# Batch 1 of a fused cross-attention and Fourier-mixing kernel: its second set of scores is turned from the first, and its steps are put in another order

## The chip, the cores and the metric

The kernel runs on one core of a Trainium2 chip. The time is device microseconds of one launch, the median of ten runs: 299.51 us, from 299.33 to 301.87. The core has five engines that each work through a list of instructions in order: TensorE (PE in the profile, its weight loads PEld), VectorE (DVE), ScalarE (ACT), GpSimd (POOL) and SyncE (SP), which here only issues DMAs. Engines wait for each other by semaphores, so an instruction that waits holds up everything behind it on its own engine.

## The reference, cut to what matters

For each of 8 batches, 8 heads of 512 rows `x` and 32 rows `state` attend to each other. The 544 result rows of 512 columns go through a two-dimensional Fourier transform, of which the real part is kept, then a normalisation and a two-layer network.

```
scores  = scale * x @ state.T        ; a  = softmax(scores)  ; xread = a  @ state    # 512 rows
scores2 = scale * state @ x.T        ; a2 = softmax(scores2) ; sread = a2 @ x        # 32 rows
X   = concat(xread, sread)           # per head; heads side by side give (8, 544, 512)
u   = X + real(fft(fft(X, axis=1), axis=2))
un  = (u - mean(u)) / sqrt(var(u) + 1e-6)
out = u + relu(un @ w_ch1) @ w_ch2   # w_ch1 512 x 2048, w_ch2 2048 x 512
```

`scores2` is the transpose of `scores`, so one exponential serves both softmaxes if it is turned.

## The kernel before, in words

Every engine's order is written out by hand; nothing is rescheduled. The kernel handles a batch in three stages, and interleaves the stages of neighbouring batches so that PE has always something to do.

**Attention** (`attend(b)`; batch 0 has its own `open_batch`). `turn_state` and `turn_x` (for batch 1 together `turn_all`, with three copies `copies1` out of PSUM) make `sT` and `xT`, the transposes of state and x. Batches from 2 on get them by DMA transposes on SP's queue (L377, L388). `scores(i)` (L432, PSUM tile `esp`) makes rows of x by columns of state and their exponential `E` on ACT (L437). The turned form `ET` is needed for `xread`. Batches from 2 on get it by `turn_scores(g)`: `E` times an identity or a mirrored identity (L444, tile `eTp`), copied by ACT with a row sum as a by-product (`sums`, L445). Batch 1 computes its scores a second time the other way round in `scores_t(g)` (L421) and takes a second exponential (L423). Then come the reads, a list called `r1` for batch 1 and `R` for batch 2. `r1[0]` and `R[0]` are `read_low` (L457 into `xrp`, a GpSimd copy `XT` at L514); index 2 and, for batch 1, 3 or 5 are the forward reads `xfp`; `sread_heads` (batch 1, L493) or `sread_by_head` (later, L477) is the state's read `srp`; `state_rows` (batch 1, L508) gathers the heads into rows; the last entry is the other mirrored read followed by the folds on DVE (L529 to L549), which make the input `XQ` of the transform. `sread_heads` takes the state's softmax sums from eight matmuls with one column each (L497).

**Transform** (`transform(b)`, list `T` for batch 2). `over_s` (L788, tile `gp`) is the transform along rows, `over_d` (L684 and L685, tile `yp`) along columns; `add`, `centre` and `turn_u` add x, subtract the mean and turn the result into `unT`, the input of the network. Batches 0 and 1 turn on PE (L856), later ones by DMA (L852).

**Network**. `layer1` is `L` for batch 0 (16 quarter steps of 16 small matmuls, L941) and `L1` for batch 1 (16 steps of 4 matmuls, L931). `layer2` gives `M` (16 steps of 4 matmuls, L996, 4 steps for each of 4 row tiles). Every fourth step of `layer2` ends with a store: DVE makes `ot` (L963), SP writes it. What is left of `M` at batch 1, `M[7]` to `M[15]`, is called `M1[0]` to `M1[8]`.

PSUM has three buffers for `esp`, `eTp`, `tp`, `gp`, `yp` and `srp` together (pool psQ), three for the network's `ph` and `po` (psF) and one pair for the reads (psX). A tile that takes a buffer waits until the one before it has been read.

One chain of orders and waits outside PE matters here. GpSimd clears and fills the state blocks of batch 2 once its DMA has landed (L168), makes the matrix `mirror` (L100, L101), issues the first half of w2 (L325, `second_weights(0, 2)`), copies and folds the low rows of batch 1 (L514 to L526), issues the second half of w2, and later casts x of batch 2 (L1123). The last four columns of that cast come only after w2's last part has landed (the read of w2 at L1181 serves for that wait). SP's DMA transposes of x of batch 2 (L388) wait for that cast, the loads of x of batch 3 stand behind these on SP's queue (L145), and GpSimd's cast of batch 3 (L148) waits for the loads. Behind that cast on GpSimd stands the copy `XT` of batch 2 (L514), and DVE may not overwrite the low rows (L484) before it is done.

Of the kernel before, what the change touches and what calls it, by code (L numbers as in the profile page):

```python
# [15 lines left out]
AF = mybir.ActivationFunctionType  # L16
# [14 lines left out]
def kernel(  # L31
# [8 lines left out]
    nc = tc.nc  # L40
    B, H, S, D = x.shape
# [316 lines left out]
    turned = {}  # L358

    def attend(b):  # L360
# [52 lines left out]
        copies = []  # L413


        def scores_t(g):
            p = qt("eTp")
            for cols, rows in ((slice(0, 128), slice(0, 128)), (slice(128, 256), slice(255, 127, -1)),
                               (slice(256, 416), slice(256, 416)), (slice(416, 512), slice(511, 415, -1))):
                for hp in range(2):  # L420
                    nc.tensor.matmul(p[:, cols], lhsT=sT[:, 2 * g + hp, :], rhs=xT[:, 2 * g + hp, rows],  # L421
                                     start=(hp == 0), stop=(hp == 1))
            nc.scalar.activation(ET[:, g, :], p, AF.Exp, scale=scale)  # L423


        def scores(i):
            p = qt("esp")
            for si in (2 * i, 2 * i + 1):
                for pr in range(4):
                    hp = pr % 2  # L430
                    o = (si % 2) * 256 + pr * 64
                    nc.tensor.matmul(  # L432
                        p[:, o:o + 64].rearrange("p (h j) -> p h j", j=Ns),
                        lhsT=xT[:, pr, si * 128:(si + 1) * 128],
                        rhs=sT[:, pr, 64 * hp:64 * hp + 64].rearrange("p (h j) -> p h j", j=Ns)[:, :, ::-1 if b < 2 else 1],
                        start=True, stop=True)
            nc.scalar.activation(E[:, 2 * i:2 * i + 2].rearrange("p a b c -> p (a b c)"), p, AF.Exp, scale=scale)  # L437

# [48 lines left out]
        def sread_heads():  # L487
            p = qt("srp")
            for g in range(2):
                for si in range(4):  # L490
                    for hh in range(4):
                        c0 = 1 + 256 * g + 64 * hh
                        nc.tensor.matmul(p[32 * hh:32 * hh + 32, 64 * g:64 * g + 64], lhsT=E[:, si, g, 32 * hh:32 * hh + 32],  # L493
                                         rhs=xin[:, si, c0:c0 + 64], start=(si == 0), stop=(si == 3))
            for g in range(2):
                for si in range(4):
                    nc.tensor.matmul(p[:, 128 + g:129 + g], lhsT=E[:, si, g, :], rhs=xin[:, si, 0:1], start=(si == 0), stop=(si == 3))  # L497
            rcs = wk.tile([128, 2], F32, name="rcs", tag="rcs")
            nc.vector.reciprocal(rcs, p[:, 128:130])
            nc.vector.tensor_tensor(XQ[:, 0:2 * D].rearrange("p (g d) -> p g d", g=2),  # L500
                                    in0=p[:, 0:128].rearrange("p (g d) -> p g d", g=2),
                                    in1=rcs.unsqueeze(2).to_broadcast([128, 2, D]), op=ALU.mult)

        def state_rows():
            p = qt("hdp")
            pv = p[0:32, :].rearrange("p (h g d) -> p h g d", h=4, g=2)
            for hh in range(4):
                nc.tensor.matmul(pv[:, hh], lhsT=ident[:, 32 * hh:32 * hh + 32], rhs=XQ[:, 0:2 * D].rearrange("p (g d) -> p g d", g=2),  # L508
                                 start=True, stop=True)
            nc.scalar.copy(XR[0:32, 0, 512:0:-1].rearrange("p (g h d) -> p h g d", g=2, d=D), pv)  # L510

# [44 lines left out]
        if b < 2:  # L556
            first = [turn_state, lambda: turn_x(0), lambda: turn_x(1)]
            if b == 1:
                first = [turn_all] + [lambda i=i: copies[i]() for i in range(3)]
            first += [lambda: scores_t(0), lambda: scores_t(1),  # L560
                     lambda: scores(0), lambda: scores(1)]
        else:
            first = [lambda: scores(0), lambda: scores(1), lambda: turn_scores(1), lambda: turn_scores(0)]
            if b >= x_by_dma:
                turned[b] = lambda: (b > 2 and turn_state(), turn_x(0), turn_x(1))
                turned[b, 0] = turn_state
            else:
                first = [turn_state, lambda: turn_x(0), lambda: turn_x(1)] + first
# [562 lines left out]
    keep_low()  # L1131
    clears(1)
    clear_state(2, 3)
    state_blocks(2, 3, nc.gpsimd.tensor_copy)
    make_mirror()
    clear_state(3, 4)
    nc.gpsimd.tensor_tensor(gate, xs_of[0][:, 0:4], w1[:, :, 3 * 512], op=ALU.add)
    second_weights(0, 2)
# [2 lines left out]
    turned[2, 0]()  # L1141
    load_state(3, 4, s_dram)
    turn_u(0, 1)
    add_sums(0, 0)
    centre_sums(0, 0)
    copies1[0]()
    copies1[1]()
    warm(4)
    L[0]()
    s1[0]()  # L1150
    copies1[2]()
    L[1]()
    turn_u(0, 0)
    s1[1]()
    add_sums(1, 1)
    centre_sums(1, 1)
    add_sums(1, 0)
    L[2]()
    s1[2]()
    r1[0]()  # L1160
    r1[1]()
    r1[2]()
    nc.gpsimd.tensor_copy(gate, xs_of[2].rearrange("p (i c) -> p i c", i=4)[:, :, 0])
    second_weights(2, 4)
    clear_state(4, B)
    L[3]()
    s1[3]()
    r1[3]()
    centre_sums(1, 0)
    L[4]()  # L1170
    r1[4]()
    r1[5]()
    turn_u(1, 1)
    L[5]()
    r1[6]()
    r1[7]()
    nc.gpsimd.tensor_copy(gate, XQs[1].rearrange("p (g j c) -> p g j c", g=2, j=4)[:, 1, 3, 0:4])
# [5 lines left out]
    turned[2]()  # L1183
    load_x(3)
    turn_in_dram(4, B)
    L[6]()
    L[7]()
    turn_u(1, 0, nc.scalar.copy)
    spread(0, 1)
    state_ones(2, B)  # L1190
    L[8]()
    L[9]()
    L[10]()
    L[11]()
    over_s1(0)
    over_s1(1)
    L[12]()
    over_s1(2)
    over_s1(3)
    keep_middle()  # L1200
    L[13]()
    over_d1(0)
    add1(0, 1)
    L[14]()
    centre1(0, 1)
    over_d1(1)
    add1(0, 0)
    L[15]()
    centre1(0, 0)
    add1(1, 1)  # L1210
    M[0]()
    turn_u1(0, 1, nc.scalar.copy)
    M[4]()
    centre1(1, 1)
    add1(1, 0)
    M[1]()
    turn_u1(0, 0, nc.scalar.copy)
    centre1(1, 0)
    M[5]()
    M[2]()  # L1220
    turn_u1(1, 1)
    M[6]()
    turn_u1(1, 0)
    spread(0, 0)
    done()
    for root in first_roots[0:1] + first_roots[5:6]:
        root()
    M[3]()
    done1()
    l2, scores_first = M, scores_next  # L1230
    for b in range(1, B + 1):
        reads_next = reads_after
        l2, l2_now = (layer2(b), [l2[7]] + l2[8:]) if b == 1 else (layer2(b) if b < B else [], l2)
        early, until, start = {2: (7, 0.25, 0.22), 3: (3, 0.13, 0.1)}.get(b, (0, 0, 0.08))
        l2_now = l2_now + (layer2(("L", b // 4)) if b in (3, 7) else [])
        streams = [(l2_now[:early], 0, until), (l2_now[early:], until + 0.02 if early else 0, 1)]
        if b == 1:
            M1, L1, R, T, s2 = l2_now, layer1(1), reads_next, transform(2), scores_first
            scores_next, reads_after = attend(3)
            s3 = scores_next  # L1240
            def spreads():
                spread(1, 1)
                spread(1, 0)
                for root in first_roots[6:8] + first_roots[1:5]:
                    root()

            for step in (M1[0], spreads, L1[0], M1[1], s2[0], s2[1], M1[2], L1[1], s2[2], s2[3], lambda: cast_x(3), turned[3], M1[3], L1[2],
                         lambda: load_state(4, B, s_dram), lambda: load_x(4), R[0], L1[3], R[1], R[2], L1[4], R[3], L1[5], R[4],
                         L1[6], R[6], L1[7], M1[4], R[7], L1[8], M1[5], M1[6], R[8], L1[9], L1[10], T[0], T[1], L1[11], T[2], T[3],
                         L1[12], T[4], L1[13], M1[7], T[5], s3[0], L1[14], T[6], s3[1], L1[15], T[7], T[8], s3[2], s3[3], T[9], T[10],  # L1250
                         T[11], M1[8], lambda: state_blocks(4, B, nc.gpsimd.tensor_copy)):
                step()
            continue
        if b < B:
            streams.append((layer1(b), start, 1))
        if b + 1 < B:
            reads, mix = {2: ((0.1, 0.45), (0.57, 0.88)), 3: ((0.03, 0.4), (0.5, 0.86))}.get(b, ((0, 0.375), (0.47, 0.85)))
            streams.append((reads_next, *reads))
            streams.append((transform(b + 1), *mix))
        if b + 2 < B:  # L1260
            scores_next, reads_after = attend(b + 2)
            streams.append(([lambda: (cast_x(b + 2), turned[b + 2]())], 0.2, 0.2))
            streams.append((scores_next, 0.5, 1))
        if b + 3 < B:
            streams.append(([lambda: load_x(b + 3)], 0.35, 0.35))
        if b in (3, 7):
            streams.append((low_rows(b // 4), 0.02, 0.2))
            streams.append((layer1(("L", b // 4)), 0.36, 0.8))
        weave(*streams)
# [30 lines left out]
```

## Time and profile before

| | |
|---|---|
| median of 10 runs | 299.51 us |
| the profiled execution, whole | 301.87 us |
| its span, first to last instruction | 300.1 us |
| PE busy | 286.7 us, 96% |
| DVE / ACT / POOL busy | 59% / 46% / 31% |
| granted TensorE clock | 1.000 |
| instructions | 6032 |

The profiled execution is the slowest of the ten runs; 1.77 us of it lie outside the span. Times in the profile count from the start of the span. An engine's row gives start and duration, and in brackets the idle time before it with the instruction or DMA that ended the wait. PE's matmuls overlap, so that a row's duration is longer than the distance to the next row; that distance is what a step costs.

### The profile page before, as it was taken

How to read it: one execution, taken by the hardware profiler on the slowest of the kernel's cores; microseconds unless marked ns; L12 is line 12 of the kernel's file. 1: busy time of each engine (PE TensorE's matmuls, PEld its weight loads, DVE VectorE, ACT ScalarE, POOL GpSimd, SP SyncE). 2: the span in 40 equal slices, each digit the busy share in tenths (PEclk: the TensorE clock that was granted, in tenths of full speed). 3: DMA queues.
4: the chain of work that ended last, by engine and by line, in shares of the span. 5: the costliest groups of instructions: out<-in, count | busy, mean ns of one | idle time of the engine just before them, and what ended most of it. 6: DMA issues, size and time to landing. Idle time of an engine off the chain costs nothing.

```text
span 300.1 us, 6032 instructions
## 1 busy us (share of the span) xinstructions
PE 286.7 (96%) x2302; PEld 164.7 (55%) x2333; DVE 178.1 (59%) x441; ACT 139.2 (46%) x258; POOL 91.8 (31%) x227
## 2 busy tenths in 40 slices
PE   5999999979899999999999999999999999999995
PEld 5789974435444655466544554455444544555443
DVE  8868987376768487645648394757568474011122
ACT  6888674635824662255423543354524443334200
POOL 6764943560580045301343033502240121000000
PEclk9999999999999999999999999999999999999999
DMA  9999993956954944574543865253332133500354
GB/s 157 191 203 189 143 168 64 181 141 142 171 119 94 207 107 72 124 171 110 91 100 72 179 123 125 52 119 75 89 88 55 37 87 90 122 14 21 98 128 126
DMA packets 110824, 34.86 MB, mean 116 GB/s; under 512 B 101980, under 2 KB 106332, under 8 KB 110796
## 3 DMA queue, kind: packets, MB, share of 16 engines
q1 hardware_dynamic: 100076, 28.72, 45.5%
q0 software_dynamic: 4224, 4.19, 9.5%
q10 hardware_dynamic: 6496, 1.57, 2.5%
q8 instruction: 18, 0.29, 0.5%
q14 instruction: 10, 0.08, 0.1%
HBM read 22.41 MB, written 14.02 MB: 121 GB/s over the span
## 4 chain that ended last, share of the span: by engine, by line
PE 75%; DMA 12%; POOL 4%; DVE 3%; SPq 2%; issue 2%; ACT 1%; ACTq 0%; POOLq 0%; DVEq 0%
PE po L996 33%; PE ph L931 32%; DMA w<-in_moe_w_ch_dram 4%; DMA s_dram<-in_state_dram 3%; PE gp L788 2%; DMA xs<-in_x_dram 2%; DMA gen<-s_dram 2%; SPq L145 2%; PE po L988 1%; PE eTp L444 1%; PE yp L685 1%; PE yp L684 1%; SPq L388 1%; DMA xT<-xin 1%; PE xrp L457 1%
## 5 line engine op out<-in xcount | busy, mean ns | idle before, releaser
L996 PE MATMUL po<-w,hT 128*128 128x512 bf16 x482 | 121.0, 379 | 1.2 <-issue 0.5
L933 ACT ACTIVATE hT<-ph 128x512 bf16<-128x512 f32 x112 | 66.9, 597 | 117.6 <-PE ph L931 113.5
L931 PE MATMUL ph<-unT,w 128*128 128x512 bf16 x431 | 112.0, 379 | 1.1 <-DVE ot L963 0.3
L931 PEld LDWEIGHTS <-w 128*128 128x128 bf16 x576 | 50.3, 98 | 46.8 <-issue 0.9
L996 PEld LDWEIGHTS <-hT 128*128 128x128 bf16 x496 | 46.7, 98 | 47.4
L963 DVE SCALAR_TENSOR_TENSOR ot<-po,rstd,U 128x512 f32<-128x512 f32 (+2 forms) x33 | 24.2, 733 | 50.4 <-PE po L996 47.9
L792 POOL COPY GL<-G 128x128 bf16<-128x128 bf16 x7 | 2.0, 289 | 73.4 <-ACT G L789 73.4
L337 DVE BATCH_NORM_STATS2 st<-U 128x6 f32<-128x512 f32 x32 | 21.8, 681 | 0.1
L689 DVE TENSOR_TENSOR U<-yp,XR 128x512 f32<-128x512 f32 x14 | 9.6, 683 | 19.9 <-PE yp L685 19.9
L344 POOL TENSOR_TENSOR rstd<-rstd,mhalf 128x1 f32<-128x1 f32 x34 | 20.0, 589 | 2.7
L343 POOL TENSOR_TENSOR rstd<-mv,epst 128x1 f32<-128x1 f32 x34 | 6.4, 189 | 44.7 <-DVE mv L339 44.7
L941 PE MATMUL ph<-unT,w 128*128 128x128 bf16 x256 | 16.2, 219 | 0.3 <-DVE unT L857 0.3
L941 PEld LDWEIGHTS <-w 128*128 128x128 bf16 x256 | 15.0, 98 | 0.5 <-issue 0.4
L789 ACT CAST G<-gp 128x288 bf16<-128x288 f32 x28 | 12.9, 482 | 5.1 <-PE gp L788 5.1
L148 POOL CAST xin<-xs 128x2048 bf16<-128x2048 f32 (+1 forms) x9 | 11.7, 1317 | 1.4 <-DMA xs<-in_x_dram 1.4
L943 ACT ACTIVATE hT<-ph 128x512 bf16<-128x512 f32 x16 | 9.5, 593 | 4.9 <-PE ph L941 4.8
L847 DVE TENSOR_SCALAR ub<-U,mv 128x512 bf16<-128x512 f32 x20 | 10.2, 511 | 0.9 <-DVE mv L339 0.3
L514 POOL COPY XT<-XR 32x514 bf16<-32x514 bf16 x7 | 4.3, 607 | 20.3 <-DVE XR L466 20.3
L466 DVE TENSOR_TENSOR XR<-xrp,rs 128x512 bf16<-128x512 f32 x14 | 9.7, 695 | 0.5
L466 DVE TENSOR_TENSOR XF<-xfp,rs 128x512 bf16<-128x512 f32 x14 | 9.7, 692 | 0.5
L465 DVE RECIPROCAL rs<-xrp 128x8 f32<-128x8 f32 x14 | 2.9, 206 | 11.2 <-PE xrp L457 11.2
L689 DVE TENSOR_TENSOR U<-yp,XF 128x510 f32<-128x510 f32 x14 | 9.4, 674 | 0.0
(245 smaller groups left out, 381.5 us busy)
## 6 DMA issues: line engine op xcount, KB each, us to landing
xs<-in_x_dram SPq DMA_DIRECT2D x22, 256.0 KB, 4.6
w<-in_moe_w_ch_dram POOLq DMA_DIRECT2D x8, 512.0 KB, 10.3
out_dram<-ot SPq DMA_DIRECT2D x15, 256.0 KB, 3.4
r_dram<-ot SPq DMA_DIRECT2D x14, 256.0 KB, 2.2
out_dram<-r_dram SPq DMA_DIRECT2D x14, 256.0 KB, 3.5
xs<-in_x_dram SPq DMA_DIRECT2D x8, 192.0 KB, 4.5
xs<-in_x_dram ACTq DMA_DIRECT2D x2, 256.0 KB
l_dram<-ot SPq DMA_DIRECT2D x2, 256.0 KB
```

The lines of the kernel that those rows point to most:

```text
L148: copy(xin_bufs[b % 2][:, lo:hi, 1:513], xs_of[b].rearrange("p (i c) -> p i c", i=4)[:, lo:hi])
L337: nc.vector.bn_stats(st6, u)
L344: nc.gpsimd.tensor_tensor(rstd, rstd, mhalf, op=ALU.pow)
L466: nc.vector.tensor_tensor(ov, in0=p[ps, :, 0:256].rearrange("p g (h d) -> p g h d", d=D), in1=rs[ps].unsqueeze(3).to_broadcast([n, 2, 4, D ...
L689: nc.vector.tensor_add(u.rearrange("p (k r) -> p k r", r=2), p.rearrange("p (r k) -> p k r", r=2)[:, 0:u.shape[1] // 2, :], x.rearrange("p ...
L789: nc.scalar.copy(G[:, j, :].rearrange("p (i q) -> p q i", q=2), p[:, 0:NM].rearrange("p (q i) -> p q i", q=2))
L847: nc.vector.tensor_scalar(t, in0=ud, scalar1=mv[:, 0:1], scalar2=None, op0=ALU.subtract)
L931: nc.tensor.matmul(ph[:, o:o + n], lhsT=w1[:, c, f * 128:(f + 1) * 128], rhs=un_of[key][:, c, :], start=(c == 0), stop=(c == DC - 1))
L933: nc.scalar.activation(hT[:, per * i:per * i + per, :].rearrange("p a b -> p (a b)"), ph, AF.Relu, scale=-1.0 / 512 if key == 0 else -1.0 ...
L941: nc.tensor.matmul(ph[:, o:o + 128], lhsT=w1[:, c, f * 128:(f + 1) * 128], rhs=un_of[key][:, c, 128 * r:128 * r + 128], start=(c == 0), st ...
L963: nc.vector.scalar_tensor_tensor(ot[:, cols], in0=po_of[i][:, 0:cols.stop - cols.start], scalar=rstd, in1=u[:, cols], op0=ALU.mult, op1=AL ...
L996: nc.tensor.matmul(po_of[i], lhsT=h_of[key][:, f, i * 128:(i + 1) * 128], rhs=w2[:, f, :], start=(f == 0), stop=(f == FC - 1))
```

## The change

Batch 1 drops `scores_t`. It computes `scores` first and turns them with `turn_scores`, as later batches do, and it takes the sums of the state's softmax from `sums`, so that the eight one-column matmuls go. The states then come out of `scores` in forward order, so `state_rows` puts them in place with slices of `mirror` in place of `ident`. `make_mirror` moves ahead of the state blocks of batch 2 on GpSimd. The three `copies1` move ahead of batch 0's second sum on DVE and ACT. The steps of batch 0's and batch 1's network, the reads of batches 1 and 2 and the stores that go with `M1[4]` and `M1[8]` are put in another order; the number of network steps stays.

```
-        def scores_t(g):
-            p = qt("eTp")
-            for cols, rows in ((slice(0, 128), slice(0, 128)), (slice(128, 256), slice(255, 127, -1)),
-                               (slice(256, 416), slice(256, 416)), (slice(416, 512), slice(511, 415, -1))):
-                for hp in range(2):
-                    nc.tensor.matmul(p[:, cols], lhsT=sT[:, 2 * g + hp, :], rhs=xT[:, 2 * g + hp, rows],
-                                     start=(hp == 0), stop=(hp == 1))
-            nc.scalar.activation(ET[:, g, :], p, AF.Exp, scale=scale)
...
-                        rhs=sT[:, pr, 64 * hp:64 * hp + 64].rearrange("p (h j) -> p h j", j=Ns)[:, :, ::-1 if b < 2 else 1],
+                        rhs=sT[:, pr, 64 * hp:64 * hp + 64].rearrange("p (h j) -> p h j", j=Ns),
...
-            for g in range(2):
-                for si in range(4):
-                    nc.tensor.matmul(p[:, 128 + g:129 + g], lhsT=E[:, si, g, :], rhs=xin[:, si, 0:1], start=(si == 0), stop=(si == 3))
             rcs = wk.tile([128, 2], F32, name="rcs", tag="rcs")
-            nc.vector.reciprocal(rcs, p[:, 128:130])
+            nc.vector.reciprocal(rcs, sums)
...
-                nc.tensor.matmul(pv[:, hh], lhsT=ident[:, 32 * hh:32 * hh + 32], rhs=XQ[:, 0:2 * D].rearrange("p (g d) -> p g d", g=2),
+                nc.tensor.matmul(pv[:, hh], lhsT=mirror[:, 96 - 32 * hh:128 - 32 * hh], rhs=XQ[:, 0:2 * D].rearrange("p (g d) -> p g d", g=2),
...
-            first += [lambda: scores_t(0), lambda: scores_t(1),
-                     lambda: scores(0), lambda: scores(1)]
+            first += [lambda: scores(0), lambda: scores(1), lambda: turn_scores(1), lambda: turn_scores(0)]
...
     clear_state(2, 3)
+    make_mirror()
     state_blocks(2, 3, nc.gpsimd.tensor_copy)
-    make_mirror()
...
     turn_u(0, 1)
+    copies1[0]()
+    copies1[1]()
+    copies1[2]()
     add_sums(0, 0)
     centre_sums(0, 0)
-    copies1[0]()
-    copies1[1]()
     warm(4)
     L[0]()
     s1[0]()
-    copies1[2]()
+    s1[1]()
     L[1]()
     turn_u(0, 0)
-    s1[1]()
     add_sums(1, 1)
-    centre_sums(1, 1)
     add_sums(1, 0)
     L[2]()
     s1[2]()
+    s1[3]()
+    centre_sums(1, 1)
+    L[3]()
+    L[4]()
     r1[0]()
     r1[1]()
     r1[2]()
...
-    L[3]()
-    s1[3]()
+    L[5]()
+    r1[4]()
     r1[3]()
     centre_sums(1, 0)
-    L[4]()
-    r1[4]()
+    turn_u(1, 1)
+    L[6]()
     r1[5]()
-    turn_u(1, 1)
-    L[5]()
+    L[7]()
     r1[6]()
     r1[7]()
...
```

From there to the loop over batches, the steps of `L` and `M` stand one or two places earlier among the steps of batch 1's transform; the order of `M` itself (0, 4, 1, 5, 2, 6, 3) stays. The loop's first pass is:

```
-            for step in (M1[0], spreads, L1[0], M1[1], s2[0], s2[1], M1[2], L1[1], s2[2], s2[3], lambda: cast_x(3), turned[3], M1[3], L1[2],
-                         lambda: load_state(4, B, s_dram), lambda: load_x(4), R[0], L1[3], R[1], R[2], L1[4], R[3], L1[5], R[4],
-                         L1[6], R[6], L1[7], M1[4], R[7], L1[8], M1[5], M1[6], R[8], L1[9], L1[10], T[0], T[1], L1[11], T[2], T[3],
-                         L1[12], T[4], L1[13], M1[7], T[5], s3[0], L1[14], T[6], s3[1], L1[15], T[7], T[8], s3[2], s3[3], T[9], T[10],
-                         T[11], M1[8], lambda: state_blocks(4, B, nc.gpsimd.tensor_copy)):
+            for step in (M1[0], spreads, M1[1], M1[2], s2[0], s2[1], L1[0], M1[3], s2[2], s2[3], L1[1], lambda: cast_x(3), turned[3], L1[2],
+                         lambda: load_state(4, B, s_dram), lambda: load_x(4), R[0], L1[3], R[1], R[3], L1[4], R[2], L1[5], M1[4], R[4],
+                         L1[6], M1[5], R[6], L1[7], R[7], L1[8], M1[6], R[8], L1[9], L1[10], M1[7], T[0], T[1], L1[11], T[2], T[3],
+                         L1[12], T[4], L1[13], T[5], s3[0], L1[14], T[6], s3[1], L1[15], T[7], M1[8], T[8], s3[2], s3[3], T[9], T[10],
+                         T[11], lambda: state_blocks(4, B, nc.gpsimd.tensor_copy)):
```

Here `s2` and `s3` are the score steps of batches 2 and 3 (two `scores`, then two `turn_scores`), `R[3]` is the state's read, `R[2]` and `R[4]` the forward reads, `R[6]` the last mirrored read.

More of the change, by code (lines that the diff above doesn't have):

```diff
@@ L1185 @@
     turn_in_dram(4, B)
-    L[6]()
-    L[7]()
+    L[8]()
+    L[9]()
     turn_u(1, 0, nc.scalar.copy)
@@ L1190 @@
     state_ones(2, B)
-    L[8]()
-    L[9]()
     L[10]()
     L[11]()
+    L[12]()
+    L[13]()
     over_s1(0)
     over_s1(1)
-    L[12]()
+    L[14]()
     over_s1(2)
@@ L1200 @@
     keep_middle()
-    L[13]()
+    L[15]()
     over_d1(0)
     add1(0, 1)
-    L[14]()
+    M[0]()
     centre1(0, 1)
@@ L1207 @@
     add1(0, 0)
-    L[15]()
+    M[4]()
     centre1(0, 0)
     add1(1, 1)
-    M[0]()
+    M[1]()
     turn_u1(0, 1, nc.scalar.copy)
-    M[4]()
     centre1(1, 1)
+    M[5]()
     add1(1, 0)
-    M[1]()
     turn_u1(0, 0, nc.scalar.copy)
     centre1(1, 0)
-    M[5]()
     M[2]()
+    M[6]()
     turn_u1(1, 1)
-    M[6]()
+    done()
+    first_roots[0]()
+    M[3]()
+    spread(0, 0)
     turn_u1(1, 0)
[L1224 to L1228, printed above, removed]
+    first_roots[5]()
     done1()
```

## The prediction

> **What bounds the kernel now.** I read the page first, then PE's waits, then the chain that ended last, then the rows around 45 to 65 us.
>
> ```profile
> span 300.1 us, 6032 instructions
> PE 286.7 (96%) x2302; PEld 164.7 (55%) x2333; DVE 178.1 (59%) x441; ACT 139.2 (46%) x258; POOL 91.8 (31%) x227
> ```
>
> PE is the bound: a saved matmul counts wherever no wait swallows it. From 28 to 90 us PE's waits are
>
> ```profile
> PE xrp L457 <- DVE XF L466: 1.6, 1, 1.6
> PE eTp L444 <- ACT E L437: 0.8, 1, 0.8
> PE gp L788 <- DVE XQ L548: 0.7, 1, 0.7
> PE esp L432 <- DMA xT<-xin: 0.4, 1, 0.4
> ```
>
> and after 90 us the list has none over 0.3 us, so what is won or lost by then stays to the end. The chain up to 54 us is not PE's:
>
> ```profile
> 28.93 1.47 POOL w L325 x2
> ...
> 36.31 10.73 DMA w<-in_moe_w_ch_dram
> ...
> 47.16 0.19 POOL gate L1181
> ...
> 51.37 2.50 DMA xT<-xin
> ```
>
> w2's transfer, a GpSimd gate, SP's transposes. The rows behind it (SP, POOL, DVE, PE) show that this chain also makes the largest wait:
>
> ```profile
> 47.52 5.12 SPq L388 DMA_TRANSPOSE xT<-xin  x4
> 52.68 5.00 SPq L145 DMA_DIRECT2D xs<-in_x_dram  x7
> ...
> 59.84 1.89 POOL L148 CAST xin<-xs 128x2048 bf16<-128x2048 f32 x1 [1.35 <-DMA xs<-in_x_dram]
> 61.67 0.61 POOL L514 COPY XT<-XR 32x514 bf16<-32x514 bf16 x1
> ...
> 62.31 1.19 DVE L484 TENSOR_TENSOR XR<-srp,rcs 32x128 bf16<-32x128 f32 x4 [1.37 <-PE xfp L457]
> 63.77 0.69 DVE L466 TENSOR_TENSOR XF<-xfp,rs 128x512 bf16<-128x512 f32 x1
> ...
> 64.52 0.40 PE L457 MATMUL xrp<-stb,ET 128*128 128x260 bf16 x2 [1.56 <-DVE XF L466]
> ```
>
> The loads of batch 3 stand behind the transposes, the cast behind the loads, `XT` behind the cast, DVE's L484 and the next `XF` behind `XT`. I call the end of `XT` X (62.28). PE's read starts at X + 2.24.
>
> **The change part by part.** Costs are distances between PE rows of the profiled execution.
>
> *Matmuls.* `scores_t` goes: 24.71 to 25.16, 0.45, twice: -0.90. `turn_scores` comes: batch 2's pair took 55.89 to 56.36: +0.47. The one-column matmuls of L497 go (29.43 to 29.65): -0.22. `state_rows` keeps four matmuls, ident or mirror. PE: -0.65. ACT pays two copies with sums (56.59 to 57.84) for two exponentials of 0.60: +0.05, beside PE's work.
>
> *Batch 1 up to its rows*, replayed from 22.26 with a quarter step at 0.89, `tp` and a read at 0.22, `scores` at 0.24. L[0] to 23.15, first scores to 23.39. The second takes the buffer of batch 0's `yp`, which DVE frees after its second sum; the `xT` copy now ahead of that sum (L411, 0.60 to the next) makes that 23.61, so PE waits 0.27. L[1], `tp`, L[2], the turned scores, L[3], L[4] bring the first read to 28.15, against 26.29. Its `ET` is ready (ACT: exponentials to 24.92, hT, two copies to 27.84). Later reads wait for DVE's `XF` 0.06 and 0.42, as DVE now has `ub` (L826) and `unT` between. L[13] ends at 38.65 with two more L than before at 37.22, that is 0.35 ahead.
>
> *The XQ wait.* DVE's folds start 1.4 later (the last read ends 33.04, not 31.63), but PE reaches them two L later, at 40.05. L548 ends at 39.2 by batch 2's rows, at 40.8 by this batch's (its L543 took 1.02, not 0.17). I take 39.9, since GpSimd's clearing of `stb` beside L543 moves 0.5 earlier: the 0.68 goes. Ends: no wait, 0.75.
>
> *M one place earlier.* DVE's normalisation of batch 1 starts 0.6 later, at 42.2, and runs dense, so two `tp` wait for `ub` 0.25 each. PE reaches batch 2's scores at 52.46, before at 53.17.
>
> *GpSimd.* `mirror` (28.21 + 0.29, 27.93 + 0.20) moves from between the state blocks' end (27.86) and w2's issue into idle time before 26.59. w2's first half is issued at 28.33, not 28.87: -0.54. `XT` of batch 1 then waits for `XR` at 29.5, not late. w2's second half is issued earlier too, but its part landed 43.5 and 47.0, behind 35.0 and 40.9 for the first half, issued 28.9 to 30.4: the transfers run one after another, and the queue, not the issue, is full. So w2, the gate, the cast, the transposes, the loads and X move by 0.54; ends: 0 (the first half meets more of the loads of x, which land until 32.2) and 1.7 (the last of w2's sixteen pieces came 1.2 after the fifteenth; with that gone too).
>
> The Trainium skill, "DMA: Bandwidth & Descriptors", section "Anatomy of one DMA — SWDGE (gpsimd) path", fits such a transfer at 2.0 us plus bytes / 436e3, an estimate of 3.2 us for 512 KB, against 10.73 in the chain above. By that rule w2 would never gate, the state blocks of batch 3 (DMA landed 44.07) would in both kernels, and moving `mirror` would win nothing: the sum below would read 0.94 slower instead of 0.40. The row decides.
>
> *Batch 2's reads.* Scores now stand behind M1[2] and before L1[0], with the same work ahead. The last transpose lands at 53.34 (53.88 - 0.54), so the second scores wait 0.7. Then L1[0] ... M1[4] bring PE to the second `xfp` at 61.8. The reads' new order puts L484 ahead of *both* `XF` on DVE, so this `xfp`, not the last `xrp`, waits for X: X is 61.74, `XF` ends 2.17 later, PE goes on at 63.96, after a wait of 2.2. Work done is that of before at 64.52, less one read. All that PE won earlier, down to 2.2 us less, is swallowed here.
>
> *Behind it.* From that start PE does: two reads 0.44, L1[6] to L1[15] and M1[5] to M1[8] 14 x 0.864, `gp` 1.13, `yp` 0.88, scores 0.48: 15.03, so the turned scores of batch 3 at 78.99. Before it was 13.92 (one read and one step less). The wait there stays. From the end of the first `yp` (74.09 before, now 74.61) to the end of the second exponential is a DVE and ACT path (L689, L337, L845, L437) of 5.33; PE's work in between is equal, as M1[8] comes where M1[7] goes. It ends at 79.94. Then a new wait: before, M1[8] and three steps (16 matmuls, 3.46) stood between the turned scores and batch 3's first read; now three steps, 2.59, so PE is there at 82.94. DVE meanwhile makes the store tile of M1[8] (0.75, 0.66 to the next) ahead of the last mean, so ACT's last `ub` starts at 81.88 (81.22 if only shifted by 0.52), `ET` follows, ready 83.78. The read ends at 83.91; before at 83.51.
>
> *Queues passed.* Root steps keep GpSimd's order. On SP, M1[8]'s store goes ahead of three of batch 2's four `unT` transposes: it waits for `ot` at 81.0, the last transpose starts 84.35 and lands 2.3 later (as the one at 82.16 did), 86.7. PE needs it at 88.1 (87.7 before). Hidden, 1.4 spare. M1[4]'s store waits for nothing behind it that is urgent.
>
> *Sum*: 63.96 - 64.52 = -0.56 at the wait for X, +0.96 behind it (19.95 against 18.99): +0.40 on the profiled span, 300.1 to 300.5. That execution took 301.87, the median 299.51; I carry the difference over: 299.9. If DMAs are faster without the profiler, both kernels see X earlier; with X 2.0 earlier, before's wait is gone, PE-bound at 62.61, after still waits, and the sum is 61.96 - 62.61 + 0.96 = +0.31.
>
> **The rivals.** *PE reaches the end of the waits (faster).* If X comes 2.9 or more earlier than in the profile, PE's own path decides: 61.09 against 62.61, -1.52, +0.96: -0.56; without the new wait for `ET` (0.84) -1.40. 298.1 to 298.9. For: plain runs are 2.4 faster than the profiled one, and the chain up to X is the part made of DMAs. Against: 2.4 is less than 2.9 and need not all lie there.
>
> *w2 does not move, or lands later.* The 0.54 is lost to the loads of x: +0.94; with another 0.5 of collision +1.4: 300.4 to 300.9. For: w2's parts land 2.6 to 5.9 apart, slowest beside SP's transposes of the state. Against: at 29.9 the large loads of x have all but landed.
>
> *The store in front of the transposes decides (slower).* On SP, transposes took 1.2 to 2.1 to issue and 2.4 to 4.0 to land. Three at 1.95 from 81.7 and a landing of 4.0 give 89.6 against 88.1: layer 1 of batch 2 starts 1.5 late, +1.9 in all, 301.4. It decides from a landing after 88.1 on, and passes the bound of measurement from 88.6. Against: the four before took 1.2 once they had data.
>
> That the change doesn't do what it says can be excluded for the matmuls: the built order has 14 matmuls and 14 weight loads less.
>
> **How the numbers follow.** A measurement of this kernel tells 0.3%, 0.9 us, from no change. Forecast as summed, -0.3 to +0.9: 0.46, nearly all of it "same" (0.42; 0.04 slower). PE's path decides: 0.26 (0.22 faster). w2 doesn't move: 0.18 (0.16 slower). The store: 0.10, slower. Faster 0.22, same 0.48, slower 0.30. The range leaves out the far half of the first and of the last rival: 298.5 to 301.1.
>
> **What would show it.** 14 matmuls fewer; w2's first issue near 28.3; no `gp` wait; an `xfp` that waits some 2 us for `XF` near 64, behind an `XT` ending near 61.7; a wait of `eTp` under 1 us; batch 3's first read waiting for ACT's `ET`. I am wrong if `XT` moves by more than 1 us against the rest, or if layer 1 of batch 2 waits for `unT`.

## The result, and the profile after

The changed kernel takes 302.45 us (302.43 to 302.93), the kernel before 299.51: 1.0082 times as long, with a 95% interval of 1.0056 to 1.0108. It is 2.94 us slower; the forecast was 299.9 and at most 301.1.

One observation frames the rest. All executions of the changed kernel lie within 0.5 us of each other. Those of the kernel before lie between 299.3 and 303.4, in some sets of runs mostly low, in one (beside `a_four` below) mostly high. Its profiled execution, 301.87, was a high one, and the changed kernel's, 302.93, is 0.5 above its usual ones. Profile against profile the difference is only 1.1 us.

The head of the changed kernel's page, with 14 matmuls less:

```profile
span 301.2 us, 6004 instructions
PE 287.0 (95%) x2288; PEld 163.8 (54%) x2319; DVE 176.8 (59%) x441; ACT 139.5 (46%) x260; POOL 90.4 (30%) x227
```

PE's waits from 20 to 95 us, the longest ones (total, number, longest):

```profile
PE xfp L447 <- DVE XF L456: 1.9, 1, 1.9
PE eTp L434 <- ACT E L427: 0.7, 1, 0.7
PE esp L422 <- DVE xT L411: 0.5, 1, 0.5
PE esp L422 <- DVE U L793: 0.5, 1, 0.5
PE xrp L447 <- DVE XF L456: 0.4, 1, 0.4
PE xrp L447 <- ACT ET L435: 0.3, 1, 0.3
```

The list looks as forecast: no `gp` wait, one large wait of the second `xfp` for `XF`, small ones for `E` and `ET`. What is behind the large one is not as forecast. The same profile's chain of work, with start and duration, walks back from that read:

```profile
50.59 0.88 PE po L982 x4
51.58 0.75 DVE ot L949
52.33 0.61 DVE st L337
52.96 0.19 DVE mv L339
...
53.49 0.56 POOL rstd L344
54.08 0.75 DVE ot L949
54.83 0.61 DVE st L337
55.47 0.20 DVE mv L339
...
55.99 0.55 POOL rstd L344
...
60.43 1.89 POOL xin L148
62.32 0.56 POOL XT L501
...
64.36 0.70 DVE XF L456
65.11 0.40 PE xfp L447 x2
```

There is no DMA in it. The transposes and loads have left the chain, and another path has come in: two output tiles (`ot`, of `M[3]` and `M[7]`) and statistics (`st`, `mv`) on DVE, then a row of root steps (`rstd`) on GpSimd, 0.78 us a pair, and only then the cast of batch 3 (`xin`), which waits for no load. In the kernel before, the same row of roots ended 1.35 us ahead of the loads in the profiled execution, and so did not show; its last root and the cast:

```profile
57.94 0.55 POOL L344 TENSOR_TENSOR rstd<-rstd,mhalf 128x1 f32<-128x1 f32 x1
59.84 1.89 POOL L148 CAST xin<-xs 128x2048 bf16<-128x2048 f32 x1 [1.35 <-DMA xs<-in_x_dram]
```

Two waits in DVE's rows of the changed kernel tell why the roots are late:

```profile
51.58 0.75 DVE L949 SCALAR_TENSOR_TENSOR ot<-po,rstd,U 128x512 f32<-128x512 f32 x1 [0.52 <-PE po L982]
52.24 0.68 DVE L337 BATCH_NORM_STATS2 st<-U 128x6 f32<-128x512 f32 x1
...
54.08 0.75 DVE L949 SCALAR_TENSOR_TENSOR ot<-po,rstd,U 128x512 f32<-128x512 f32 x1 [0.63 <-POOL rstd L344]
```

The first `ot` waits for PE, which is late. The statistics of `spread(0, 0)`, which the change put behind `M[3]` (the section on the change does not list this move), come after it, their root after them, and the second `ot` waits for that root. The last two statistics, and the roots behind them, wait for the second `ot`. In the kernel before, the second `ot` waits 0.28 for a root.

### The profile page after: what moved, and what is told of

Read it like the earlier page. It is cut to its first block, busy times and chain, and to the rows that moved or that the text cites. A ratio compares the mean times of both kernels' runs of the same rounds, so it can differ in the third digit from the quotient of the medians.

```text
span 301.2 us, 6004 instructions
## 1 busy us (share of the span) xinstructions
PE 287.0 (95%) x2288; PEld 163.8 (54%) x2319; DVE 176.8 (59%) x441; ACT 139.5 (46%) x260; POOL 90.4 (30%) x227
## 4 chain that ended last, share of the span: by engine, by line
PE 80%; DVE 10%; POOL 3%; ACT 2%; issue 2%; DMA 1%; POOLq 0%; DVEq 0%; ACTq 0%
PE po L982 32%; PE ph L917 30%; PE ph L927 4%; PE gp L774 2%; DVE st L337 2%; DVE U L675 1%; PE yp L670 1%; PE yp L671 1%; PE po L974 1%; POOL rstd L344 1%; DVE ot L949 1%; PE xrp L447 1%; DMA gen<-in_state_dram 1%; PE eTp L434 1%; PE esp L422 1%
## 5 line engine op out<-in xcount | busy, mean ns | idle before, releaser
L427 ACT ACTIVATE E<-esp 128x512 bf16<-128x512 f32 x14 | 8.2, 596 | 4.4 <-PE esp L422 4.3
```

## The experiments

**Theory A**: GpSimd's queue, roots ahead of the cast of batch 3, sets `XT` (X in the forecast) in the changed kernel. It is late for two reasons, PE's waits in batch 1 and the place of `spread(0, 0)`. **Rivals**: the loads set `XT` in both kernels (B); PE's own time, not `XT`, is lost (C). Comparisons with the changed kernel are with its 302.45, which was timed in one set of runs only; `a_late_copy` below, whose edit moves next to nothing, took 302.38 in another.

**Roots between cast and `XT`, a badly placed test.** In both kernels:

```diff
-                for root in first_roots[6:8] + first_roots[1:5]:
+                for root in first_roots[6:8]:
                     root()
...
+            def cast_then_roots():
+                cast_x(3)
+                for root in first_roots[1:5]:
+                    root()
...
-... lambda: cast_x(3), turned[3], ...
+... cast_then_roots, turned[3], ...
```

> The changed kernel, with GpSimd's cast of batch 3 ahead of the four root steps of batch 1 (they are needed only by batch 1's layer 2). Theory A, the roots hold the cast: in the changed kernel's profile GpSimd is dense from 55.73 to the end of the cast at 62.3, six root pairs of 0.78 ahead of a cast whose data are there. With two pairs instead of six ahead of it the cast can start at 57.3, or when the loads have landed (about 57.7); XT ends near 60.2, not 62.9, and PE's wait for XF of 1.9 us goes: 1.5 to 1.9 faster than the changed kernel, 300.6 to 301.0. Theory B, the loads of batch 3 hold the cast in both kernels: nothing moves, 302.4. Theory C, PE lost its time before 54 us and waits only because it is late: also faster, as A, but with 1 us or more left against the kernel before in the start of the next stage.

> The same edit to the kernel before: its six root pairs ended 1.35 us before the loads had landed. Theory A (roots hold the cast only in the changed kernel): 299.5, within 0.5. If the roots hold the cast in the kernel before as well when its loads come sooner (roots end 58.5, XT then at 61.0 at the earliest, PE's own path needs 60.4 for no wait): up to 0.6 faster, 298.9. Theory B: the same as before, 299.5.

Measured: 305.71 and 305.50 us, 1.0196 (1.0166 to 1.0226) and 1.0172 (1.0136 to 1.0208) times the kernel before. In the changed kernel the cast did start earlier (57.78; in the other it waited for its loads until 58.92), but the four roots then stood between it and `XT`, which ended at 63.4 and 64.5. Both expectations missed that it is `XT`, not the cast, that PE needs. GpSimd's order thus does matter, in the kernel before too once roots stand behind a late load. The size needs a second cause. PE's wait grew from 1.9 to 2.9 us in the changed kernel, 1 us, but the time by 3.3 (2.8 in the profiled execution, 305.20). A table by stretch of the changed kernel with this edit (stretch, its length, busy us and count of PE, PEld, DVE, ACT, POOL, then the granted TensorE clock, DMA share, GB/s):

```profile
64.00:65.00 1.00, 0.00 (x0) 0.00 (x0) 0.92 (x4) 0.00 (x0) 1.00 (x4) 1.00 0.30 66
...
66.00:67.00 1.00, 1.00 (x5) 0.40 (x4) 0.97 (x3) 0.00 (x0) 0.41 (x2) 0.71 0.49 99
67.00:68.00 1.00, 1.00 (x4) 0.41 (x3) 0.04 (x1) 0.60 (x1) 0.00 (x0) 0.50 1.20 135
68.00:69.00 1.00, 1.00 (x5) 0.43 (x3) 0.00 (x0) 0.00 (x0) 0.00 (x0) 0.50 0.53 96
69.00:70.00 1.00, 1.00 (x5) 0.43 (x4) 0.63 (x2) 0.00 (x0) 0.00 (x0) 0.58 0.37 76
```

After the wait the clock is halved for some 3.4 us; by these means that is a loss of about 1.7 us on top of the wait.

**Roots behind the folds.** The same in both kernels, with the four roots behind `R[1]`, where nothing urgent waits:

```diff
-                for root in first_roots[6:8] + first_roots[1:5]:
+                for root in first_roots[6:8]:
                     root()
+            def roots():
+                for root in first_roots[1:5]:
+                    root()
...
-... R[1], R[3], L1[4], ...      # before: R[1], R[2], L1[4]
+... R[1], roots, R[3], L1[4], ...
```

> The changed kernel, with the four root steps of batch 1 behind GpSimd's folds of batch 2, so that only two root pairs stand ahead of the cast and none between the cast and XT. (With the roots between the cast and XT, XT came 0.5 later than in the changed kernel, and PE waited 2.9 us for XF at a cost of 3.3 us: the clock fell to 0.66 behind that wait.) Theory A, GpSimd's queue sets XT: the cast starts with its loads at about 57.8, XT ends at 60.3 instead of 62.9, the wait for XF of 1.9 us goes to 0 to 0.4: 1.5 to 1.9 faster than the changed kernel's 302.45, 300.5 to 301.0. Theory B, the loads set it in most executions: 302.4. Theory C, the reads of batch 2 meet another late producer (DVE's XR, ot) at nearly the same time: 0.5 faster or less, 302.0.

> The same for the kernel before. Its roots end at 58.5 at the latest, in the profiled execution 1.35 us ahead of the loads; in executions whose loads come sooner they would set XT at 61.0. Theory A: 299.0 to 299.5, that is at most 0.5 faster than before, and no change in executions with late loads. If it gains over 1 us, GpSimd held the kernel before as well and the changed kernel's loss is not in the later roots alone.

Measured: the changed kernel 300.84 us (300.36 to 302.22), 1.6 less than without the edit; the kernel before 300.46 against 300.22 in runs beside it, 0.9981 (0.9947 to 1.0015), no difference. GpSimd's rows of the first:

```profile
56.30 0.55 POOL L344 TENSOR_TENSOR rstd<-rstd,mhalf 128x1 f32<-128x1 f32 x1
57.86 1.89 POOL L148 CAST xin<-xs 128x2048 bf16<-128x2048 f32 x1 [1.02 <-DMA xs<-in_x_dram]
59.70 0.60 POOL L501 COPY XT<-XR 32x514 bf16<-32x514 bf16 x1
```

Now the cast waits for its loads, as in the kernel before, `XT` is 2.6 earlier than in the changed kernel's profile (2.1 without that execution's late start, below), and PE has no wait for `XF` at the `xfp`. The spread of times has come back as well: the loads decide again. A against B is settled: the roots hold `XT` in the changed kernel, the loads in the profiled execution of the kernel before. In its shortest executions neither costs much: without the four roots ahead of the cast the lowest time is 299.23, with them 299.33.

**The counter-test: hold the cast in the kernel before.** Tiny copies on GpSimd ahead of the cast:

```diff
                 for root in first_roots[6:8] + first_roots[1:5]:
                     root()
+                for _ in range(14):          # b_late_small: 6
+                    nc.gpsimd.tensor_copy(gate, w2[:, 12:16, 0])
```

> The kernel before, with 14 tiny copies (128x4 into the gate tile, about 0.14 us each by their spacing in the trace, 2.0 us in all) on GpSimd behind its roots and ahead of the cast of batch 3. They stand in for what the change did to that queue. Undisturbed, the roots of the kernel before end near 57.6; the cast then starts at 59.6, XT ends at 62.05, PE's last read of batch 2 starts 2.24 later at 64.3 instead of 62.2. Theory A (GpSimd's place alone accounts for most of the loss): 301.4, between 301.0 and 302.0, and the executions lie close together, as they do for the changed kernel, since the loads no longer decide; with a wait over 2 us the clock may fall as well, then 302 to 303.5. Theory C (PE's own lateness ahead of M[7] is what costs): 299.5 to 300.2, spread as before.

> The kernel before with 6 of the tiny copies ahead of the cast instead of 14. The 14 took 3.43 us, not 2.0, and PE's wait of 3.85 brought the clock down. 6 take 1.47: the cast starts at 59.1, XT ends at 61.6, PE's last read starts at 63.85 instead of 62.2, after a wait of about 1.8, as in the changed kernel, and without a fall of the clock. Theory A: 301.1, within 0.3, and runs close together unless loads come later than 59.1. Theory C (GpSimd's queue is not what costs): 299.5 to 300.

Measured: 305.22 us with 14, 301.28 (lowest 301.04) with 6, 1.0173 (1.0141 to 1.0205) and 1.0028 (0.9998 to 1.0059) times the kernel before, whose executions beside the second have a median of 300.35 and a lowest of 299.34. The 14 were sized wrong: a copy took 0.245, not 0.14, PE waited 3.85, and the clock fell to 0.5. With 6 the cast starts at 59.28 and PE's last read of batch 2 where it was expected:

```profile
59.28 1.89 POOL L148 CAST xin<-xs 128x2048 bf16<-128x2048 f32 x1
63.96 0.40 PE L457 MATMUL xrp<-stb,ET 128*128 128x260 bf16 x2 [2.27 <-DVE XF L466]
```

Lowest against lowest, a later cast alone makes the kernel before 1.7 us slower, over half of the 3.1 between it and the changed one. By medians it is 0.9, which the interval does not tell from none, as the kernel before has late loads of its own in many executions.

**Why the roots are late: the order at the end of the block.**

```diff
     done()
-    first_roots[0]()
-    M[3]()
     spread(0, 0)
-    turn_u1(1, 0)
+    first_roots[0]()
     first_roots[5]()
+    M[3]()
+    turn_u1(1, 0)
     done1()
```

> The changed kernel with the statistics of batch 0's second block, spread(0, 0), and its root ahead of M[3], as in the kernel before; the rest as changed. In the changed kernel's trace the ot of M[7] waits 0.63 for this root, whose statistics stand behind M[3]'s ot on DVE, and the last root pairs wait for statistics behind M[7]'s ot. Theory A1 (this reordering, not PE's lateness, makes most of the roots' delay): M[7]'s ot starts when its matmuls end, 1.0 to 1.3 earlier, and the roots, the cast and XT with it: 301.2 to 301.6. Theory A2 (PE's lateness ahead of M[7] makes nearly all of it): 302.0 to 302.4. Theory B (loads): 302.4.

Measured: 301.39 us (most executions 301.2 to 301.6), 1.06 less than the changed kernel. The second `ot` starts without a wait and the cast at 58.73 (59.94 to 60.00 in two kernels below that keep the changed order here):

```profile
52.38 0.75 DVE L949 SCALAR_TENSOR_TENSOR ot<-po,rstd,U 128x512 f32<-128x512 f32 x1
...
58.73 1.89 POOL L148 CAST xin<-xs 128x2048 bf16<-128x2048 f32 x1
```

So moving one statistics step and its root behind `M[3]` cost 1.1 us.

**Why the roots are late: PE's waits in batch 1.** Three tests: DVE's copy of `xT` later; layer 1's `L[1]` ahead of the scores; and the kernel before with the new form of the scores and as few moved steps as it needs.

```diff
+++ a_late_copy, against the changed kernel
     copies1[1]()
-    copies1[2]()
     add_sums(0, 0)
     centre_sums(0, 0)
+    copies1[2]()
+++ a_l1_first, against the changed kernel
     L[0]()
+    L[1]()
     s1[0]()
     s1[1]()
-    L[1]()
+++ b_scores, against the kernel before: functions of the changed kernel, mirror first, and
+    copies1[2]()
     warm(4)
     L[0]()
     s1[0]()
-    copies1[2]()
...
     s1[2]()
+    s1[3]()
+    L[3]()
     r1[0]()
...
-    L[3]()
-    s1[3]()
     r1[3]()
```

> The changed kernel with DVE's copy of xT behind the second sum of batch 0 and its centring instead of ahead of them. In the changed kernel's profile PE waits 0.49 for that copy, which itself waits for ACT's, and 0.45 for the sum behind it. Theory A (what PE loses ahead of M[7] comes back one for one through ot, the roots, the cast and XT): the second wait goes, the first grows by DVE's 0.6 to 1.2 for the sum: between 0.5 faster and 0.7 slower, and the end moves by just as much as M[7]'s last matmul does. Theory B: the early waits are covered, 302.4 whatever they do.

> The changed kernel with L[1] ahead of the two score steps of batch 1 instead of behind them. L[1] takes 0.89, so PE's waits for xT (0.49) and for the sum (0.45) have cover. Theory A (what PE loses ahead of M[7] passes one for one through ot, the roots, the cast and XT): M[7], the roots and XT move 0.7 to 0.95 earlier, the loads at 57.8 do not yet bind: 301.5 to 301.8. If what follows cannot use it (the chain from E over the turn to ET becomes the wait ahead of the first reads): 302.0 to 302.5. Theory B (the loads hold the cast): 302.4.

> The kernel before with the new form of the scores and the mirror ahead of the state blocks, but as few steps moved as the form needs: both score steps, then both turns, layer 1's step L[3] and then the first reads; the matrix steps behind, and the loop over b == 1, as before. Theory A, the loss is in the order of the steps up to M[7]: PE does 0.65 less work, waits about 0.4 for ET, reaches M[7] as before (about 53.2), the roots end near 58.5, and what remains is what the mirror alone showed (301.55, with executions from 299.95 to 304.8): 299.5 to 301.5. Theory C, the form itself costs (its chain from E over the turn to ET): PE waits over 1 us ahead of the first reads, or later, and the time is 302 or more.

Measured: 302.38 (302.33 to 302.59), 302.15 and 302.75 us. The late copy traded one wait for the other (1.0 for `xT`, none for the sum) and M[7] moved by 0.1 at most; nor did the time. `L[1]` first brought half of what was expected: M[7]'s `ot` 0.4 earlier, the cast 0.4 earlier, 0.3 to 0.4 off the time. That is one for one, as theory A has it. `b_scores` came out as theory C had it, at over 302; its largest waits, of which the last is batch 2's wait for `XT`:

```profile
PE xfp L447 <- DVE XR L456: 1.2, 2, 1.0
PE esp L422 <- DVE xT L411: 1.0, 1, 1.0
PE xrp L447 <- DVE XF L456: 1.0, 1, 1.0
```

PE waits over 2 us ahead of M[7], 1.0 for `xT` and 1.0 for the buffer that `XR` frees among them. Next to their old places the turned scores are late for the reads: the way from `xT` leads over `E`, the turn and two copies to `ET`, before over one exponential. But this is not the price of the form alone. `L[3]` and a score step, which stood between the first two reads, stand ahead of both here, so that nothing covers the second wait; the mirror's move is in it; and the cast starts at 60.87, 0.44 behind its last root, with the loads' last issue at 58.0 (54.9 in the changed kernel with the roots behind the folds). How much of PE's loss in batch 1 is the form's and how much the order's was not separated.

**The mirror alone.**

```diff
+    make_mirror()
     state_blocks(2, 3, nc.gpsimd.tensor_copy)
-    make_mirror()
```

> The kernel before, with the mirror made ahead of the state blocks, the only piece of the change that stands alone. The step of my forecast: w2 is issued 0.54 earlier, the cast's data come 0.5 to 1.7 earlier, so 0.3 to 0.5 faster where the loads hold the cast, 299.0 to 299.2, and in the profiled execution the wait of 1.6 for XF shrinks to 1.1 or less. Theory A: in most executions the loads do not hold it, so the time stays, 299.5 within 0.3, and only the longer executions (300.7 to 303.2) become fewer.

Measured: 301.55 us (299.95 to 304.82), 1.0049 (1.0012 to 1.0085): slower, not 0.3 to 0.5 faster. In its profiled execution (300.11) w2 is issued 0.65 earlier than in the kernel before with the roots behind the folds (27.35 against 28.00), but GpSimd's gate opens later. Its rows in the two kernels, this one first:

```profile
43.56 1.26 POOL L168 CAST stb<-gen 32x128 bf16<-32x128 f32 x4 [2.73 <-DMA gen<-s_dram]
44.89 0.19 POOL L1181 CAST gate<-w 128x4 f32<-128x4 bf16 x1
```

```profile
41.40 1.26 POOL L168 CAST stb<-gen 32x128 bf16<-32x128 f32 x4
44.04 0.19 POOL L1181 CAST gate<-w 128x4 f32<-128x4 bf16 x1 [1.37 <-DMA w<-in_moe_w_ch_dram]
```

With w2 ahead, the state of batch 3 (`gen`, issued at 37.66 instead of 34.15) lands later, and it now holds the gate. That the earlier transfer pushed back the other is a reading of one execution of each; in the profiled execution of the kernel before, with w2 issued at 28.87, `gen` was issued at 36.53. What makes single executions reach 304 us was not seen, since a low one was profiled.

**The loop over b == 1.** The whole old list in the changed kernel, and two pieces of it:

```diff
+++ a_old_list: the whole list of steps of the kernel before
+++ a_m8_last
-... L1[15], T[7], M1[8], T[8], s3[2], s3[3], T[9], T[10], T[11], ...
+... L1[15], T[7], T[8], s3[2], s3[3], T[9], T[10], T[11], M1[8], ...
+++ a_old_reads
-... R[1], R[3], L1[4], R[2], L1[5], M1[4], R[4], ...
+... R[1], R[2], L1[4], R[3], L1[5], M1[4], R[4], ...
```

> The changed kernel, with the order of steps of the loop over b == 1 (layer 1 of batch 1, layer 2, reads of batch 2, transform of batch 2) as before. Theory A: M[7], on which the roots wait, stands before this list, so XT stays near 62.9 and the wait for XF of about 1.9 stays, now at the last xrp; behind it the last output block of batch 0 goes back to the end of the stage, and the waits for E and ET (0.7 and 0.3) shrink: 0.3 to 1.2 faster than the changed kernel, 301.2 to 302.1. Theory C, the list holds the loss: 299.5 to 300.0.

> The changed kernel with the last output step of batch 0, M1[8], back at the end of the stage, nothing else. With the whole old list the changed kernel took 301.82. My forecast put +0.96 on this part: one step less between the turned scores of batch 3 and its first read, and M1[8]'s ot on DVE ahead of the last mean, so that PE waits for E and then for ET. If that step is right, 0.3 to 0.65 faster than the changed kernel, 301.8 to 302.1, with no wait of xrp for ET. If the 0.65 came from the order of the reads or of layer 1 instead: 302.4 or slower.

> The changed kernel with the old order of batch 2's reads alone: the two reads of XF before and after the score read stand as before, so DVE makes the first XF ahead of the rows that wait for XT. The whole old list gave 0.65, the last output step alone lost 0.45, so the rest should hold 1.1. If the reads hold it, as in my forecast (two XF behind XT instead of one): XT stays, PE's wait moves from the second xfp to the last xrp with one read and one step more done by then: 0.6 to 1.1 faster, 301.3 to 301.9. If M1[4] to M1[7] and L1 hold it instead: 302.4.

Measured: 301.82, 302.95 and 301.25 us. (One execution of the first, the profiled one, took 1514.66 us at a granted clock of 0.19; no profile of it is read.) `M1[8]` at its old place makes it 0.3 (lowest) to 0.5 (median) slower: its four matmuls stand ahead of the turned scores of batch 3 and hide part of the wait for `E`, which grows from 0.7 to 1.7, in two waits, without them. That is the opposite of the forecast's +0.96. The reads alone give 1.2, so that the two make up the list's 0.65: in their old order the second `xfp` does not wait for `XT`, PE does the read, `L1` and `M1` steps behind it meanwhile, and the wait that is left stands at the last read:

```profile
62.91 0.39 PE L447 MATMUL xfp<-stb,ET 128*128 128x260 bf16 x2
65.28 0.40 PE L447 MATMUL xrp<-stb,ET 128*128 128x260 bf16 x2 [0.26 <-DVE XF L456]
```

**Together.** `a_three` is `a_l1_first`, the roots behind the folds and the old list; `a_four` is `a_l1_first`, `a_old_tail`, the roots behind the folds and `a_old_reads`.

> The changed kernel with three edits together: L[1] ahead of batch 1's scores, the four roots behind the folds of batch 2, and the old order of the loop over b == 1. Theory A: the gains add, as they lie one behind the other: from 300.84 (roots alone) 0.7 to 0.9 for the early waits, as far as the loads allow, and 0.65 for the list: 299.3 to 299.8 in executions with early loads, so no slower than the kernel before and up to 0.7 faster than its runs on the same chip (299.3 to 303 so far). Theory C (the new form of the scores costs PE time that no order here gives back): 300.2 or more, slower than the kernel before.

> The changed kernel with four pieces put right at once: L[1] ahead of batch 1's scores (gave 0.3), batch 0's second statistics ahead of M[3] (1.1), the four roots behind the folds (1.6), the old order of batch 2's reads (1.2). Theory A: the last three shorten one and the same wait of 1.9 to 2.3 us, so they don't add: XT is then set by the loads (cast from 57.8), PE waits no more, and what stays is what PE loses ahead of batch 2's scores (53.4 against 52.4 in the kernel before): 300.0 to 300.5, still 0.6 to 1.0 over the kernel before's undisturbed 299.35. If they add: 298.3 or less, faster than the kernel before.

Measured: 301.27 and 300.73 us (lowest 301.17 and 300.44; the second is 0.2 above its expected range). `a_three` missed by 1.5: the old list has a step of layer 1 of batch 1 directly behind M[7], and PE waits 0.98 there for `unT`, whose copy stands behind `M[3]`'s `ot` and the statistics of `spread(0, 0)` on DVE. A step that was covered in one order was not covered in the mixed one. `a_four` shows that the pieces are one wait counted several times: alone they gave 1.6, 1.2, 1.1 and 0.3, together 1.7. It waits for no `XT` any more, and what is left against the low executions of the kernel before (300.44 against 299.38) is what PE loses in batch 1: batch 2's scores start at 53.63, and at 52.38 in the kernel before with the roots behind the folds. That is theory C's share, about 1 us. Beside it the kernel before took 301.32, mostly in its longer executions; the ratio of 0.9991 (0.9965 to 1.0017) tells no difference. No version here is shown to be faster than the kernel before.

## Why the prediction was wrong

**What bounds it** was read rightly for the execution that was profiled: PE's wait for `XT`, `XT` behind the loads. What was not seen is that GpSimd's roots ended only 1.35 us ahead of those loads, in plain sight in its rows, and that with loads 2 us sooner the two are about level.

**Matmuls, batch 1, the XQ wait, M one place earlier.** No `gp` wait and the waits for `E` and `ET` came as forecast, the last two smaller (below). Batch 2's scores were forecast at 52.46 and start at 53.81 (without the late start of the profiled execution, whose PE is 0.48 behind at its first `L` step already). The replay from 22.26 let DVE start its copy of `xT` at 22.1; it waits 0.92 for ACT's, and PE waits 0.49 for it, then 0.45 for the sum behind it and 0.40 at the last read, where nothing, 0.27 and 0.42 were put down. By the starts of the rows the second scores come at 24.68 (same allowance) instead of 23.61, which is 1.07 of the 1.35.

**GpSimd.** w2's earlier issue was real; that the gate, the transposes, the loads and X follow by 0.54 was not shown: by itself the edit is 1.4 slower by medians, and in its profiled execution the gate opens later.

**Batch 2's reads: the step that failed.** It set X at 61.74, as before less 0.54. X is the later of loads and roots, and the roots moved the other way. The sentence "Root steps keep GpSimd's order" is true and beside the point: each root waits for statistics on DVE, and these had been put behind an `ot` that waits for PE. X ended at 62.88; in executions without the profiled one's late start it is 62.4, against 60.1 for roots that end at 57.7, as they do ahead of the 6 copies above. Of these 2.3, 1.2 is the place of `spread(0, 0)`, and the remaining 1.0 is put down to PE's lateness. That a wait of 2.2 follows at the second `xfp` was right (1.9), and the order of the reads makes it cost 1.2.

**Carrying the profile's excess over.** The sum was made against a profiled execution 2.36 above the median, and all of that was taken off the forecast. The excess lay in the very waits that the change rebuilt: the low profiled execution of the kernel before with the roots behind the folds (299.23) reaches the last read of batch 2 at 62.2, not 64.5. The changed kernel's GpSimd chain holds no DMA, so nothing comes off there but the 0.48 of its start. That is 1.9 of the error of 2.55; the other 0.66 is the profiled difference, +1.06 instead of +0.40. Its first term, -0.56 at the wait for X, came out as +0.59 (the read starts at 65.11, not 63.96), its second, +0.96, as +0.47.

**Behind it, and the queues.** +0.96 was the sum of one step less and one `ot` more. PE's waits for `E` and `ET` there were put at 0.95 and 0.84 and are 0.74 and 0.29; `M1[8]`'s place turned out to win 0.3 to 0.5. SP's store ahead of the transposes cost nothing: no layer 1 step waits for `unT` there, as forecast.

**The rivals.** "PE reaches the end of the waits" was right that X is about 2 earlier in usual executions of the kernel before, and wrong that the changed kernel follows. "w2 does not move" had the right sign for the mirror. None named GpSimd's roots.

## What to carry to other kernels

When a wait goes, look at what on the same in-order queue ended just before it: its slack is the limit of any gain, and once it is delayed by more than that, it is the bound. A small step (statistics, a root) that is moved behind an instruction that waits for PE can delay everything that is queued behind its consumer on a third engine. And a profiled execution's excess over the median may be taken off a forecast only where the waits that make it are left as they were.

## What the runs showed of the hardware

In the profiled executions a wait of PE of 2.27 us (the 6 copies) left the granted clock at 1.0; waits of 2.85, 3.85 and 5.07 brought it to 0.5 for about 3.4 to 6.8 us, and the fall came 3.5 to 3.8 us after the wait had begun (worked out from the mean clock of each stretch of 1 us): in the table above PE had been at work again for 0.8 us. Mean clocks of all six executions of that kernel were 0.987 to 0.994. So the step from a wait of 1.9 us to one of 2.9 cost more than twice its length.

The Trainium skill, "TensorE: Matmul & The Clock Gate", Part 1, says that the array falls to half its rate after an idle window of about 3.4 us in a free-running count. Half the rate is what the rows show; that a wait shorter than this window sufficed is what they add.
